# Block attention and a gated MLP on one core: tokens turned by VectorE, row numbers loaded for four query blocks at once, and a new table for the order

## The chip, the cores and the metric

One core of a Trainium2 chip runs the whole program. The metric is the device time of one execution in microseconds (us); less is better. Times of the kernel before are a median of three runs. The profile is one execution, and its trace gives every instruction's engine, source line, start and length.

## What is computed

The reference, cut to what matters (4 batches, 8 heads, 768 tokens, 64 per head; blocks of 32 tokens; 512 model columns, 2048 hidden):

```python
mask = np.abs(blk_i - blk_j) <= 1
mask = mask | (blk_i == 0) | (blk_j == 0) | (blk_i == n_blocks - 1) | (blk_j == n_blocks - 1)
for qb in range(n_blocks):
    for kb in sampled_blocks[qb]:          # three drawn blocks of keys for each block of queries
        mask[qb*32:(qb+1)*32, kb*32:(kb+1)*32] = True
attn = softmax(where(mask, q @ k.T / 8, -1e9)) @ v
x = attn, heads side by side                # 3072 x 512
h = x @ w_in
g = h * np.tanh(np.where(h > 20.0, h, np.log1p(np.exp(np.minimum(h, 20.0)))))
out = g @ w_out
```

The weights arrive as 64-bit floats and are read as pairs of 32-bit words.

## The kernel before, in words

**The work.** Attention goes in 52 jobs, 13 for each batch: one job for query block 0, one for block 23 (these two are dense, they see all keys) and eleven of two neighbouring query blocks each. A job of two blocks runs like this, by the functions in `attend` and around it. `gather_k` copies the keys of the three drawn blocks, whose numbers are only known when the program runs, into the tile `kg` (POOL or ACT, line 588 or 590). `gather_v` fetches the rows of v from the DRAM tensor `vd` into the tile `vg` by DMAs that SyncE (SP) issues (lines 607 to 613). PE multiplies the scores `s` (line 650 in batch 0, which is computed in 32-bit floats; line 660 in the others, where each number is two 16-bit halves). DVE takes their maxima `mx` (line 703), ACT the exponentials `pt` (line 729). The probabilities are turned, by PE in batch 0 (`t`, line 749) and by a transposing DMA in the others (line 784), after a split into halves `p` (lines 773, 775, 780). PE multiplies with v into `o` (lines 814, 830) and DVE divides by the sums into `xs` (lines 851 to 866).

**The turn of the tokens.** `xs` holds 32 queries of four pairs of heads in its 128 partitions. For the MLP the 512 columns have to lie in partitions. Before, `tx_fn` (line 884) does this with one PE product by the identity for each query block, into a PSUM tile `tx`; ACT copies it to 16 bits (`xh`, line 902) and DVE writes what is left (`xl`, line 905).

**The MLP.** Twelve tiles of 256 tokens. PE multiplies `h` from `xh`, `xl` and the split weights `wi` (line 1083; 12 instructions make one unit, 192 units in all) and `y` from `g` and `wo` (line 1143; 6 instructions make one unit, 192 in all). Between them stand, on `[128, 1024]` tiles, the copy `hs` (ACT, line 1092), exponential, square and logarithm `us` (lines 1106 to 1115; the square on POOL, line 1112, or ACT, line 1113), the product `hs` (DVE, line 1116), its 16-bit half `g` (line 1124 or 1122) and the rest of it (POOL, line 1127, or DVE, line 1129). A tile of `h` needs `xh` and `xl` of eight query blocks: job 4 of a batch completes its first tile, job 8 the second, job 12 the third.

**The row numbers.** `blocks_at` (line 562) loads numbers of drawn blocks from an SBUF table into registers of the engine that needs them, by a TENSOR_LOAD (line 567), and keeps them while the next call asks for the same group. A group is one job: two query blocks, six numbers. Each of POOL, ACT and SP has registers of its own.

**What sets the order.** `Plan` (line 41) lists all tasks with their engines, assumed durations, the tiles they read and write and a number `key`. `emit` goes through them as a list scheduler: it takes the task that can start first and, among those that start within 0.02 us, the one with the least ready time plus key. Some tasks have several engines and go to the one that would be done first by the plan. MLP products go in a fixed order of their own. `START` gives the first 18 jobs a time before which their scores count as late, and `RES` an amount of MLP work to be kept for the end. In idle time that the plan foresees on PE in the first 150 us it puts products of zeros (line 918). What each engine executes is then this order, in sequence: an instruction that waits holds up all behind it on its engine. Tiles are taken from rings of fixed size (`RINGS`); PSUM ring `t` has two places, shared by `t`, `tx` and small sums.

## Time and profile before

| | us |
|---|---|
| median of 3 runs | 736.8 |
| lowest and highest of them | 735.41, 741.06 |
| the profiled execution | 739.81 |
| its span in the trace | 737.8 |
| PE, DVE, ACT, POOL busy in the span | 695.8, 577.3, 517.1, 269.9 |

The span runs from the first to the last instruction that the profiler recorded. Busy time counts an engine's instructions without gaps and without waits; register loads, branches and the issuing of DMAs are not in it. "Idle before, releaser" names what ended the wait ahead of an instruction. SPq, ACTq and POOLq are the engines' instruction queues. PEclk is the granted clock of TensorE as a share of 2.4 GHz.

### The profile page before, as it was taken

The page shows a single profiled execution, that of the slowest core. Times are in us where ns is not written, and L with a number is a line of the kernel's source. Part 1 is how long each engine was busy: PE and PEld are TensorE (multiplying, and loading weights), DVE is VectorE, ACT ScalarE, POOL GpSimd, SP SyncE. Part 2 cuts the span into 40 slices and gives each one's busy share as a digit, 9 for nine tenths or more (in the row PEclk, how much of TensorE's full clock was granted, in tenths as well). Part 3 has the DMA queues.
Part 4 walks back from the last instruction along what each step waited for, and adds up shares of the span by engine and source line. Part 5 has one row for each costly group of instructions (what it writes and reads, how often), then busy time and mean ns, then how long its engine had stood idle before and what let it go on. Part 6 is the DMA issues. An engine that isn't in the chain of part 4 may idle for free.

```text
span 737.8 us, 25470 instructions
## 1 busy us (share of the span) xinstructions
PE 695.8 (94%) x10462; PEld 462.3 (63%) x10462; DVE 577.3 (78%) x1064; ACT 517.1 (70%) x841; POOL 269.9 (37%) x330
## 2 busy tenths in 40 slices
PE   9988898999999799998999999998999999999997
PEld 3645776775565376765567666665666666676653
DVE  3788899789988567896969999999899887354350
ACT  3466697998888658877558888877677876464550
POOL 2264453554436232462427554355433511000000
...
GB/s 273 365 207 246 263 208 245 139 132 30 204 145 146 185 154 168 126 238 167 123 135 158 135 215 208 141 187 203 130 175 139 116 137 137 167 65 15 15 15 28
DMA packets 144599, 115.94 MB, mean 157 GB/s; under 512 B 96739, under 2 KB 107492, under 8 KB 144484
## 3 DMA queue, kind: packets, MB, share of 16 engines
q1 hardware_dynamic: 144288, 114.06, 61.5%
...
q14 instruction: 33, 0.27, 0.1%
q10 hardware_dynamic: 196, 0.27, 0.1%
...
## 4 chain that ended last, share of the span: by engine, by line
PE 53%; DVE 17%; DMA 14%; SPq 6%; ACT 5%; issue 4%; POOL 0%; ACTq 0%; DVEq 0%
PE y L1143 22%; PE h L1083 20%; DMA vg<-vd 8%; DMA wr<-in_moe_w_in_dram 3%; PE s L660 3%; PE o L830 3%; SPq L613 3%; DVE p L780 2%; DVE p L775 2%; DVE hs L1116 2%; DMA raw_q<-in_q_dram 2%; DVE mx L703 2%; PE o L814 1%; SPq L567 1%; PE tx L884 1%
## 5 line engine op out<-in xcount | busy, mean ns | idle before, releaser
L1083 PE MATMUL h<-xh,wi 128*128 128x256 f16 x1536 | 284.0, 274 | 0.0
L1143 PE MATMUL y<-wo,g 128*128 128x512 f16 x1152 | 277.4, 382 | 3.6 <-DVE ys L1156 3.6
L1083 PEld LDWEIGHTS <-wi 128*128 128x128 f16 x2304 | 222.5, 98 | 52.8 <-issue 3.4
L1083 PE MATMUL h<-xl,wi 128*128 128x256 f16 x768 | 210.0, 273 | 0.0
L1143 PEld LDWEIGHTS <-g 128*128 128x128 f16 x1152 | 111.0, 99 | 111.0 <-issue 9.8
L588 POOL COPY kg<-kt 128x256 f16 (+1 forms) x213 | 106.6, 542 | 112.7 <-PE s L660 82.3
L729 ACT ACTIVATE pt<-s,nb,ns 128x256 f32<-128x256 f32 (+1 forms) x208 | 105.4, 577 | 4.1 <-DVE nb L718 1.9
L1127 POOL TENSOR_TENSOR g<-hs,g 128x1024 f16<-128x1024 f32 x30 | 67.5, 2250 | 110.6 <-DVE g L1124 39.1
L1092 ACT ACTIVATE hs<-h,gsc 128x512 f32<-128x512 f32 x96 | 65.5, 684 | 59.3 <-PE h L1083 58.8
L1116 DVE SCALAR_TENSOR_TENSOR hs<-us,hs 128x1024 f32<-128x1024 f32 x48 | 61.6, 1284 | 22.5 <-ACT us L1115 22.1
L1112 POOL TENSOR_TENSOR us<-us 128x1024 f32<-128x1024 f32 x27 | 53.5, 1980 | 67.5 <-DVE us L1110 62.2
L780 DVE SCALAR_TENSOR_TENSOR p<-pt,p 128x512 f16<-128x512 f32 (+1 forms) x102 | 73.5, 749 | 1.4 <-ACT p L773 0.6
L775 DVE TENSOR_SCALAR p<-pt 128x512 f16<-128x512 f32 (+1 forms) x68 | 49.0, 740 | 11.5 <-ACT pt L729 8.2
L703 DVE TENSOR_REDUCE mx<-s 128x4 f32<-128x1024 f32 x44 | 53.3, 1212 | 4.8 <-PE s L650 3.0
L1106 ACT ACTIVATE us<-hs,hsc 128x1024 f32<-128x1024 f32 x48 | 55.2, 1151 | 1.3
L1114 ACT ACTIVATE us<-us 128x1024 f32<-128x1024 f32 x48 | 50.7, 1057 | 4.7 <-POOL us L1112 4.0
L1110 DVE TENSOR_SCALAR us<-us 128x1024 f32<-128x1024 f32 x48 | 34.1, 710 | 23.0 <-ACT us L1106 23.0
L1115 ACT ACTIVATE us<-us 128x1024 f32<-128x1024 f32 x48 | 50.7, 1056 | 0.9
L830 PEld LDWEIGHTS <-pp 128*32 128x32 f16 x2952 | 33.6, 97 | 24.4 <-issue 14.0
L830 PE MATMUL o<-vg,pp 128*32 128x65 f16 (+2 forms) x2568 | 36.0, 205 | 9.0 <-DMA vg<-vd 8.7
L590 ACT ACTIVATE kg<-kt 128x256 f16 (+1 forms) x51 | 15.6, 368 | 33.3 <-POOL kg L588 9.8
L918 PE MATMUL zeros<-z 128*128 128x512 f16 x136 | 35.0, 405 | 4.0 <-issue 2.3
...
## 6 DMA issues: line engine op xcount, KB each, us to landing
...
```

The source lines that it names most:

```text
L588: nc.gpsimd.tensor_copy(out=dst, in_=src)
L703: nc.vector.tensor_reduce(out=mx.rearrange("p g w -> p (g w)"), in_=tl[ks].rearrange("p g (w k) -> p (g w) k", k=KT), axis=AX.X, op=ALU.max)
L729: ex = lambda o, x, g, w: nc.scalar.activation(out=o, in_=x, func=AF.Exp, bias=nb[:, g, w:w + 1], scale=ns(w)[:, 0:1])
L775: nc.vector.tensor_scalar(out=h16[:, cs], in0=src, scalar1=PSC, scalar2=None, op0=ALU.mult)
L780: nc.vector.scalar_tensor_tensor(out=x[:, 1, cs], in0=src, scalar=PSC, in1=x[:, 0, cs], op0=ALU.mult, op1=ALU.subtract)
L830: nc.tensor.matmul(o[cs, at] if v1 == VW else o[cs, at, 0:v1 - v0], p[:, k, g, cs], x, start=j == 0 and g == 0 and k == 0 and n == 0, stop ...
L1083: nc.tensor.matmul(h[:, f2].rearrange("p (s q) -> p s q", q=BS), wi[:, fp, w, cc, fs], x[:, :, cc], start=f2 == 0 and k == 0, stop=f2 == 1 ...
L1092: nc.scalar.activation(out=tl[kq][:, 2 * (fp % 2):2 * (fp % 2) + 2], in_=tl[kh], func=AF.Copy, scale=gsc[:, fp:fp + 1])
L1106: nc.scalar.activation(out=new(sb, "us", ku, [P, 4, TT]), in_=hs(), func=AF.Exp, scale=hsc[:, b:b + 1])
L1116: add("DVE", 1.32, lambda: nc.vector.scalar_tensor_tensor(out=hs(), in0=us(), scalar=-0.5, in1=hs(), op0=ALU.add, op1=ALU.mult), r=[ku], w ...
L1127: add("POOL", 2.3, lambda: nc.gpsimd.tensor_tensor(out=g()[:, 1], in0=hs(), in1=g()[:, 0], op=ALU.subtract), r=[kq, ("gh", b, t, k)], w=[k ...
L1143: nc.tensor.matmul(tl[ky], tl["g", b, t, k][:, g, f, q], wo[:, fc, w], start=fc == 0 and n == 0, stop=fc == NFC - 1 and n == 2)
```

## The change

Five things change.

- `tx_fn` is now one DVE instruction for a job (STREAM_TRANSPOSE, turning each block of 32x32), from `xs` into an SBUF tile `tx` with a ring of one place. A column of the 512 ends in another partition than before, and `load_i` takes the rows of w_in in the matching order. The ring of `xs` has one place instead of two.
- `xh` may be made by ACT, POOL or DVE, `xl` by POOL or DVE, as the plan finds it.
- `blocks_at` loads the numbers of four query blocks (12 registers) at once, the last group of a batch two; a group now serves two jobs.
- Every key is looked up in a table `PRIO` by task and batch; `START` and `RES` have other numbers.
- The plan's assumed durations are others, and compute tasks get a small latency by engine (`LAT`).

```diff
-             xs=2, hs=3, us=3, g=4, ys=1, kt=1, q=2, ssk=2, ssv=2, ssq=2, sck=2, scv=2, scq=2, iv=2, ns=3, ws=2,
-             wq=2, am=2, p16=3)
+             xs=1, hs=3, us=3, g=4, ys=1, kt=1, q=2, ssk=2, ssv=2, ssq=2, sck=2, scv=2, scq=2, iv=2, ns=3, ws=2,
+             wq=2, am=2, p16=3, tx=1)
+PRIO = {
+    "zeros": (-1475,),
...
+    "tx": (-80.3, 357.3, -117, -301.3),
...
+}
+def K(name, n):
+    row = PRIO[name]
+    return row[min(n, len(row) - 1)]
+LAT = {"ACT": 0.11, "DVE": 0.08, "POOL": 0.06}
...
+        lat = lat or LAT.get(eng, 0.0)
...
-            n = 2 * NR
+            n = min(4, NB - 1 - qb) * NR
...
         def tx_fn():
-            tx = new(ps["t"], "t", ("tx", i), [P, nsu, P])
-            for w in range(nsu):
-                nc.tensor.transpose(tx[:, w], tl["xs", i][:, w].rearrange("p g d -> p (g d)"), ident)
-        add("PE", 0.25, tx_fn, r=[("xs", i)], w=[("tx", i)], new=[("t", ("tx", i))], key=-3 + (-63 if b == 0 else -7), lat=0.25, kind=("X", i))
+            tx = new(sb, "tx", ("tx", i), [P, nsu, NCC, BS])
+            xs = tl["xs", i].rearrange("p w g d -> p w (g d)").rearrange("p w (d c) -> p w c d", c=NCC)
+            nc.vector.transpose(tx if nsu > 1 else tx[:, 0], xs if nsu > 1 else xs[:, 0])
+        add("DVE", 0.45 if nsu > 1 else 0.3, tx_fn, r=[("xs", i)], w=[("tx", i)], new=[("tx", ("tx", i))], key=K("tx", b))
...
-            run(lambda x, hi, lo: nc.scalar.activation(out=hi, in_=x, func=AF.Copy))
-
-        def xl_fn():
-            run(lambda x, hi, lo: nc.vector.tensor_tensor(out=lo, in0=x, in1=hi, op=ALU.subtract))
+            if eng == "ACT":
+                run(lambda x, hi, lo: nc.scalar.activation(out=hi, in_=x, func=AF.Copy))
+            else:
+                run(lambda x, hi, lo: (nc.vector if eng == "DVE" else nc.gpsimd).tensor_copy(out=hi, in_=x))
+
+        def xl_fn(eng):
+            run(lambda x, hi, lo: (nc.vector if eng == "DVE" else nc.gpsimd).tensor_tensor(out=lo, in0=x, in1=hi, op=ALU.subtract))
...
-        src = w_in.rearrange("(c p) f -> p c f", p=P)[:, :, k * 2 * P * W:(k + 1) * 2 * P * W]
+        src = w_in.rearrange("(p c) f -> p c f", p=P)[:, :, k * 2 * P * W:(k + 1) * 2 * P * W]
...
-            su["first"] = job["sus"][0]["qb"]
+            su["first"] = su["qb"] - (su["qb"] - 1) % 4
...
-    RES, START = 152, [75, 143, 351, 1, 289, 59, 444, 40, 4, 303, 106, 133, 87, 206, 53, 166, 65, 18]
+    RES, START = 142.9, [0, 2.2, 0.9, 28.4, 939.4, 56.8, 14.9, 34.5, 18.6, 102, 75.8, 71.8, 144.1, 1792, 50.5, 27.1, 193.2, 56.8]
```

Where instructions stand, at three places. In a name, `s_17` is the score tile of job 17, `tx_14` the turned tokens of job 14, `h_0_2_3` piece 3 of tile 2 of batch 0; a number at the end counts buffers.

PE in batch 1, behind the scores of job 17, before:

```order
L660 LDWEIGHTS q_1_1_3804
L660 MATMUL s_17_4148<-kg1_110,q_1_1_3804 32x256
L884 MATMUL tx_14_4202<-ident_64,xs_14_4123 128x128 x2
L1143 LDWEIGHTS g_0_1_0_3305
L1143 MATMUL y_0_1_1_4096<-wo_72,g_0_1_0_3305 128x512
```

and now:

```order
L756 LDWEIGHTS q_1_1_3624
L756 MATMUL s_17_4126<-kg1_110,q_1_1_3624 32x256
L1244 LDWEIGHTS g_0_1_2_3534
L1244 MATMUL y_0_1_0_3839<-wo_72,g_0_1_2_3534 128x512
...
L1184 LDWEIGHTS wi_71
L1184 MATMUL h_0_2_3_4008<-xh_0_2_2307,wi_71 128x256
```

The 96 products `tx` are gone from PE's sequence, 9 of which stood ahead of the first MLP product. Job 17's scores now stand at MLP unit 60 of 384, before at unit 68.

SP, from the gather of v for job 4 (its first block goes to `vg0`, its second to `vg1`), before:

```order
L607 DMA vg0_111<-vd0_60 96x520
L567 TENSOR_LOAD offv_87
...
L607 DMA vg1_112<-vd0_60 96x520
...
L931 DMA wor_0_1196<-in_moe_w_out_dram 128x1024
L931 DMA wor_1_1203<-in_moe_w_out_dram 128x1024
L931 DMA wor_2_1255<-in_moe_w_out_dram 128x1024
L931 DMA wor_3_1259<-in_moe_w_out_dram 128x1024
```

and now:

```order
L703 DMA vg0_111<-vd0_60 96x520
...
L1032 DMA wor_0_1189<-in_moe_w_out_dram 128x1024
L1032 DMA wor_1_1197<-in_moe_w_out_dram 128x1024
L1032 DMA wor_2_1234<-in_moe_w_out_dram 128x1024
L1032 DMA wor_3_1238<-in_moe_w_out_dram 128x1024
L1032 DMA wor_4_1250<-in_moe_w_out_dram 128x1024
L1032 DMA wor_5_1279<-in_moe_w_out_dram 128x1024
L703 DMA vg1_112<-vd0_60 96x520
```

Job 4 needs no load of its own any more (job 3's serves it), and six pieces of w_out of 512 KB each are issued between the fetches for its two blocks.

DVE, around the division and the turn of job 4, which completes the first tile of x, before:

```order
L945 SCALAR_TENSOR_TENSOR wi_71<-wr_7_895,wi_71 128x1024
L851 TENSOR_SCALAR r_4_1308<-o_4_1205,iv_r_114 128x4
L855 RECIPROCAL r_4_1308<-r_4_1308 128x4
L866 TENSOR_TENSOR xs_4_1311<-o_4_1205,r_4_1308 128x256
L939 TENSOR_SCALAR wo_72<-wor_0_1196 128x512
```

and now:

```order
L1159 TENSOR_SCALAR hsc_81<-gmx_77,iv_x_78 128x1
L1043 SCALAR_TENSOR_TENSOR wo_72<-wor_4_1250,wo_72 128x512
L1046 SCALAR_TENSOR_TENSOR wo_72<-wor_1_1197,wo_72 128x512
L1040 TENSOR_SCALAR wo_72<-wor_5_1279 128x512
L947 TENSOR_SCALAR r_4_1527<-o_4_1256,iv_r_114 128x4
L951 RECIPROCAL r_4_1527<-r_4_1527 128x4
L962 TENSOR_TENSOR xs_4_1530<-o_4_1256,r_4_1527 128x256
L980 STREAM_TRANSPOSE tx_4_1572<-xs_4_1530 128x256
```

Before, job 4's division followed the last decode of w_in at once; now it stands behind the scales of the MLP (`hsc` is the last of them) and three more instructions that decode w_out.

## Rows read from the trace of the kernel before

**Rows 1.** The chain of work that ended last, its shares by line.
```profile
PE y L1143 22%; PE h L1083 20%; DMA vg<-vd 8%; DMA wr<-in_moe_w_in_dram 3%; PE s L660 3%; PE o L830 3%; SPq L613 3%; DVE p L780 2%; DVE p L775 2%; DVE hs L1116 2%; DMA raw_q<-in_q_dram 2%; DVE mx L703 2%; PE o L814 1%; SPq L567 1%; PE tx L884 1%
```

**Rows 2.** Stretches: length, then busy us of each engine, PEclk, DMA share, GB/s.
```profile
0.00:79.70 79.70, 67.23 (x1092) 39.77 (x1093) 57.83 (x124) 43.59 (x87) 31.88 (x52) 0.97 0.85 271
79.70:140.00 60.30, 55.83 (x1045) 44.48 (x1046) 53.53 (x99) 48.45 (x80) 24.68 (x25) 0.98 0.74 228
140.00:640.00 500.00, 478.95 (x7596) 319.22 (x7595) 430.44 (x795) 382.42 (x628) 213.35 (x255) 0.99 0.68 155
sum 738.00, PE 695.84 PEld 462.25 DVE 577.33 ACT 517.06 POOL 269.92; mean PE 173.96 PEld 115.56 DVE 144.33 ACT 129.27 POOL 67.48
...
400.00:480.00 80.00, 77.90 (x1229) 52.91 (x1228) 77.89 (x140) 66.84 (x112) 39.48 (x37) 1.00 0.77 172
```

**Rows 3.** The same stretches, PE line 884 alone: the sum.
```profile
sum 738.00, PE 20.63 PEld 11.70; mean PE 5.16 PEld 2.92
```

**Rows 4.** PE in order of time, 236 to 262 us: start, length, instructions.
```profile
240.17 4.05 PE L1143 MATMUL y<-wo,g 128*128 128x512 f16 x18
...
250.63 0.69 PE L884 MATMUL tx<-ident,xs 128*128 128x128 f32 x2 [1.49 <-DVE xs L861]
251.11 5.33 PE L1143 MATMUL y<-wo,g 128*128 128x512 f16 x12
```

**Rows 5.** Instructions on the tile tx: ns min/median/max.
```profile
L902 ACT ACTIVATE xh<-tx x60: 255/363/412, 36.4 to 661.2; 128x256 f16<-128x256 f32 x36, 128x128 f16<-128x128 f32 x24
L905 DVE TENSOR_TENSOR xl<-tx,xh x60: 269/410/426, 37.1 to 661.6; 128x256 f16<-128x256 f32 x36, 128x128 f16<-128x128 f32 x24
```

**Rows 6.** Groups by line and shape: busy us, mean ns | idle before.
```profile
L1129 DVE TENSOR_TENSOR g<-hs,g 128x1024 f16<-128x1024 f32 x18 | 22.0, 1224 | 0.5
L775 DVE TENSOR_SCALAR p<-pt 128x512 f16<-128x512 f32 x46 | 37.2, 818 | 11.1 <-ACT pt L729 7.9 <-DMA pp<-p 3.1
L590 ACT ACTIVATE kg<-kt 128x256 f16 x33 | 11.3, 405 | 17.9 <-PE s L660 8.2 <-issue 3.2 <-PE o L830 2.2
L1113 ACT ACTIVATE us<-us 128x1024 f32<-128x1024 f32 x21 | 22.2, 1056 | 8.6 <-DVE us L1110 8.3
L1112 POOL TENSOR_TENSOR us<-us 128x1024 f32<-128x1024 f32 x27 | 53.5, 1980 | 67.5 <-DVE us L1110 62.2 <-DVE iv_x L396 3.8 <-DVE iv_k L396 1.6
L1127 POOL TENSOR_TENSOR g<-hs,g 128x1024 f16<-128x1024 f32 x30 | 67.5, 2250 | 110.6 <-DVE g L1124 39.1 <-ACT g L1122 31.8 <-PE o L830 11.3
```

**Rows 7.** DVE line 775 and ACT line 773: ns min/median/max.
```profile
L775 DVE TENSOR_SCALAR p<-pt x68: 278/424/2256, 176.6 to 624.2; 128x512 f16<-128x512 f32 x46, 128x256 f16<-128x256 f32 x22
...
L773 ACT ACTIVATE p<-pt x34: 399/621/647, 178.3 to 625.3; 128x512 f16<-128x512 f32 x20, 128x256 f16<-128x256 f32 x14
```

**Rows 8.** The register loads of line 567: ns min/median/max.
```profile
L567 POOLq TENSOR_LOAD <-offk x44: 1384/1388/2469, 7.9 to 584.4; - x44
L567 SPq TENSOR_LOAD <-offv x44: 1264/1286/2340, 35.3 to 647.8; - x44
L567 ACTq TENSOR_LOAD <-offk x17: 1324/1337/2686, 8.7 to 598.2; - x17
```

**Rows 9.** DVE in order of time, 58 to 84 us.
```profile
71.07 0.42 DVE L866 TENSOR_TENSOR xs<-o,r 128x256 f32<-128x256 f32 x1
...
77.86 0.20 DVE L1058 TENSOR_SCALAR hsc<-gmx,iv_x 128x1 f32<-128x1 f32 x1
```

**Rows 10.** PE in order of time, 58 to 84 us.
```profile
75.09 0.27 PE L1083 MATMUL h<-xh,wi 128*128 128x256 f16 x1
...
78.35 0.32 PE L814 MATMUL o<-vg,pp 128*32 128x65 f32 x8 [1.79 <-DMA vg<-vd]
...
79.61 0.39 PE L1083 MATMUL h<-xh,wi 128*128 128x256 f16 x1
```

**Rows 11.** The chain between 40 and 84 us, in order of time.
```profile
66.01 1.14 PE s L650 x62
67.15 0.59 PE t L749 x4
...
73.28 5.51 DMA vg<-vd
```

More of the change, by code (lines that the diff above doesn't have):

```diff
@@ L381, in diag @@
                                            accum_out=out())
-        add("DVE", 0.4, diag, r=[kg], w=w, new=new_, key=cls + 12)
+        add("DVE", 0.4, diag, r=[kg], w=w, new=new_, key=K("diag " + ring, 0))
     def root_pe(key, ss, apart):
@@ L437, in load @@
         add("SP", 0.5 * n, fn, r=after, w=keys,
-            new=[(ring, key) for key in keys], key=(-5 if b == 0 else 0) + (0 if b == 0 else 59), lat=1.8,
+            new=[(ring, key) for key in keys], key=K("load " + what, j if b == 0 else len(T3)), lat=1.8,
             kind=("dma", 1.5 * n, n))
@@ L448, in fn @@
             squares(tl["raw", what, b, j], tl[key][:, k:k + 1])
-        add("ACT", 1.28, fn, r=[("raw", what, b, j)], w=[key], new=[(f"ss{what}", key)] if first else (), key=cls + 47 + (19 if b == 0 else 19))
+        add("ACT", 1.05, fn, r=[("raw", what, b, j)], w=[key], new=[(f"ss{what}", key)] if first else (), key=K("ss " + what, j if b == 0 else len(T3)))
     def scales(b, what, j, cls):
@@ L532, in fn @@
                 (nc.vector if eng == "DVE" else nc.gpsimd).tensor_copy(out=dst, in_=src)
-        add("POOL", 0.3, ends, w=[("ends",) + key], new=[("raw", key)], use=[key], key=-2)
-        add("DVE", 0.8, lambda: fn("DVE"), r=[kr, ("ends",) + key], w=[key], use=[key], key=ATV + 94, port=True,
-            also=[("ACT", 1.16, lambda: fn("ACT")), ("POOL", 2.0, lambda: fn("POOL"))])
+        add("POOL", 0.3, ends, w=[("ends",) + key], new=[("raw", key)], use=[key], key=K("ends0", 0))
+        add("DVE", 0.67, lambda: fn("DVE"), r=[kr, ("ends",) + key], w=[key], use=[key], key=K("copy v", j), port=True,
+            also=[("ACT", 1.05, lambda: fn("ACT")), ("POOL", 1.05, lambda: fn("POOL"))])
     def store_v(b, j):
@@ L719, in nb_fn @@
                                             op0=ALU.mult)
-        add("ACT", 0.25 * len(wq), lambda: nb_fn("ACT"), r=[kmx] + NS, w=[("nb", i)],
-            new=[("nb", ("nb", i))], key=45.5 + (21 if b == 0 else -20), also=[("DVE", 0.35 * len(wq), lambda: nb_fn("DVE"))])
+        add("ACT", 0.19 * len(wq), lambda: nb_fn("ACT"), r=[kmx] + NS, w=[("nb", i)],
+            new=[("nb", ("nb", i))], key=K("nb", b), also=[("DVE", 0.15 * len(wq), lambda: nb_fn("DVE"))])
         def ex_fn(n):
@@ L738, in attend @@
         for n in range(2):
-            add("ACT", 1.7 if dense and n == 0 else 1.15, lambda n=n: ex_fn(n),
+            add("ACT", 1.33 if dense and n == 0 else 0.91, lambda n=n: ex_fn(n),
                 r=[kmx, ("nb", i), ks] + (k2 if dense else []) + NS,
-                w=[("p", i, n)], new=[("pt", k) for k in kps] if n == 0 else (), use=kps, key=-1.5 + (-3 if b == 0 else 54))
+                w=[("p", i, n)], new=[("pt", k) for k in kps] if n == 0 else (), use=kps, key=K("ex", b))
         def t_fn(j):
@@ L1053, in fn @@
             nc.vector.tensor_scalar(out=gsc, in0=iv_i, scalar1=rg, scalar2=-2.0 * GSC, op0=ALU.mult, op1=ALU.mult)
-        add("DVE", 0.7, fn, r=[("iv", k) for k in range(0, NFP, 2)], w=["gsc"], key=27)
+        add("DVE", 0.7, fn, r=[("iv", k) for k in range(0, NFP, 2)], w=["gsc"], key=K("gsc", 0))
     def scales_b(b):
@@ L1093, in hs_fn @@
                                  scale=gsc[:, fp:fp + 1])
[L1094 to L1095 removed]
+        add("ACT", 0.58, hs_fn, r=[kh, "gsc"], w=[("hsw", b, t, fp)],
+            new=[("hs", kq)] if fp % 2 == 0 else (), use=[kq], key=K("hs", b))
         if fp % 2 == 1:
@@ L1201, in attn_mish_kernel @@
     add("ACT", 1.0, lambda: which(new), w=["off", "z"],
-        new=[("raw", ("z",))], key=-6, lat=6.0)
+        new=[("raw", ("z",))], key=K("which", 0), lat=6.0)
     globals_(0)
@@ L1259, in attn_mish_kernel @@
         if i == LAST:
-            add("PE", 0.0, spare.clear, r=["zeros", ("begun", i)], use=[("zeros",)], key=-982)
+            add("PE", 0.0, spare.clear, r=["zeros", ("begun", i)], use=[("zeros",)], key=K("clear", 0))
         if b + 1 < B:
```

217 lines of the change are left out of this document (141 added, 76 removed), and 16 rows, old and new, of the table PRIO.

## The prediction

> **What bounds the kernel now.** I read the chain of work that ended last first, then the busy time of each engine by stretches, then single places in order of time, then groups of instructions and register loads. In the chain the reader is to see that the two MLP products of PE hold 42% of the span and that no line of DVE or ACT holds over 2% [rows 1]. The stretches say the same [rows 2]: from 140 to 640 us PE is busy 478.95 of 500, so it idles 21.0; from 79.7 to 140 it idles 4.5; in the first 79.7 us it works on little but prepared weights, the first jobs and zeros while DMA moves 271 GB/s. PE is the bound from its first MLP product on. DVE is the next: 57.8 + 53.5 + 430.4 = 541.8 us busy up to 640, and 77.89 of 80 between 400 and 480, where PE nevertheless has 77.90 of 80 [rows 2]. ACT has 474.5 of 640. So a microsecond taken from PE is worth nearly a microsecond as long as DVE and ACT can deliver the same work in a shorter time.
>
> **The change part by part.** The sum is made against the profiled execution: 739.8 us, that is the span of 737.8 and 2.0 around it. The median of the runs is 736.8, 3.0 lower; I move every result by that.
>
> *The turn leaves PE.* Line 884 takes 20.63 us of PE [rows 3] in 96 products, 0.215 each. Nine stand ahead of the first MLP product, where PE has time to spare; the other 87 stand where PE is the bound: 87 x 0.215 = 18.7 us less. Nothing on PE takes their place, all its other products keep their number except 17 more zeros ahead of the MLP. I take the whole 18.7.
>
> *Waits ahead of the turn leave PE too.* PE executes in order, so a turn that waits for DVE's division holds up the MLP products behind it. At 250.63 it waited 1.49 us, and the 12 `y` products behind it took 5.33 us, where 18 took 4.05 just before, which is 2.70 for 12: 2.63 more [rows 4]. This place alone costs 4.1 us. The others are short, and the wait may come back at a product `h` that needs the last `xl`; but the places of job 17's scores show that jobs now run some 8 MLP units ahead of where they ran. I take 4 us less; the ends are 0 and 8, twice this place.
>
> *What DVE gets.* 44 turns of 256 columns and 8 of 128. No row shows this operation. The nearest rows are `xl` on the same elements, 0.410 and 0.269 at the median and the least [rows 5]: 44 x 0.410 + 8 x 0.269 = 20.2 us. From below I bound it by 52 x 0.278, the least of line 775 [rows 7], 14.5; from above by 52 x 0.818, the mean of its wide form [rows 6], 42.5. I take 20.2, the row with the same shape. A turn can't cost less than nothing on an engine that didn't have it. Against it, `xl` goes to POOL in 53 of 60 cases: 31 x 0.410 + 22 x 0.269 = 18.6 less. The new order also gives DVE 14 more of line 1129 (32 for 18), 14 x 1.224 = 17.1 more [rows 6], takes 11 wide and 8 narrow of line 775 away, 11 x 0.818 + 8 x 0.278 = 11.2 less [rows 6, 7], and adds 8 `xh`, 8 x 0.41 = 3.3 more. The other differences go both ways, none over 5 us; I count them nothing. DVE: 20.2 - 18.6 + 17.1 - 11.2 + 3.3 = 10.8 more, 552.6 of about 620 us, 89%. This lies beside PE's work and costs nothing while that cover holds.
>
> On VectorE's turn the Trainium skill (VectorE: DVE Perf Modes, section on the three transpose paths) has 311 ns for 128x128 in 16 bits, and blocks of 32x32 only. By that, as an estimate, the 96 blocks would be 29.9 us, and DVE would be 20.5 us up instead of 10.8; no run here shows its price, and the forecast stays the same by either.
>
> What DVE may get back: the wide form of line 775 takes 0.818 on average, while the median of both forms is 0.424 and the longest 2.256 [rows 6, 7]; POOL's long operations take 1.98 and 2.25 [rows 6]. An operation of 0.4 that takes the time of POOL's looks like one that had to wait for it: 46 x 0.394 = 18.1 us in this group. Of those POOL operations 27 are left of 57 (lines 1112 and 1127: 11 and 16, before 27 and 30). I count no gain, but this is a reason why DVE should not become the bound.
>
> *What POOL and ACT get.* POOL loses 16 x 1.98 + 14 x 2.25 = 63 us and 75 copies of keys and gains 88 short operations on 256 columns at most; at even 0.8 each they are 70. It has 270 of 738 and isn't near the end of any wait that PE sees. ACT gets the 75 copies, 75 x 0.405 = 30.4 more, 16 squares, 16 x 1.056 = 16.9 more [rows 6], 19 scalings that DVE gave up, 19 x 0.621 = 11.8 more [rows 7], and 43 fewer `xh`, 26 x 0.363 + 17 x 0.255 = 13.8 less [rows 5]. That is 45.3 more: 519.8 before the last job ends. Hidden at 84% of 620 us, with what follows.
>
> *Register loads.* POOL and ACT now have 23 each, SP 24; before 44, 17 and 44. A load of six numbers takes 1.388, 1.337 and 1.286 us [rows 8] and the engine issues nothing in that time. A load of twelve isn't in the trace: between the same time (the cost is that of one access) and twice that (it is by the number). At the same time SP saves 20 x 1.286 = 25.7 us and ACT loses 6 x 1.337 = 8.0. At twice, SP has 24 x 2.57 = 61.7 for 56.6 and ACT 23 x 2.67 = 61.5 for 22.7. Behind a load on SP stand fetches of v that PE waits for: 8% of the chain is that DMA and 1% the load itself [rows 1]. I take the middle, nothing gained or lost: half of the jobs are free of the load and the other half pay more. The ends: 5 us less (the load's share in the chain, 1% of 738, of which half goes) to the rival below.
>
> *The start.* The first MLP product now needs more. Job 4's division stood at 71.07 [rows 9] and the first product came 4.0 us later, at 75.09; after one unit PE waited for job 5's v and went on with `h` at 79.61 [rows 10], so the MLP began, in effect, at 79.6 - 1.3 = 78.3. Now the division stands behind `hsc`, which ended at 78.06 [rows 9], and three decodes of some 0.4 to 0.8 us. That makes xs about 80.1 and the first product 84.1, 5.8 later. Ahead of it PE has then done more: job 7's scores, 1.14, both turns of job 6, 2 x 0.59 [rows 11], and half a product of job 5, 0.3: 2.6 us. 5.8 - 2.6 = 3.2; I take 3 us more. The ends: 2 less, if the two loads saved ahead of job 4's fetch on SP (2 x 1.286) pull the whole start; 6 more, if its second fetch waits behind six pieces of w_out, 6 x 0.524 MB at 271 GB/s = 11.6 us (a fetch behind four took 5.51 [rows 11]): 71.07 + 11.6 + 4.0 - 78.3 - 2.6 = 5.8.
>
> *The rest of the order* (keys, START, RES, places in the rings `xs` and `tx`) I can't price line by line. A single `tx` and a single `xs` bind a job's division to the `xl` of the job before, some 10 us earlier in the MLP stages; I count nothing.
>
> The sum: -18.7 - 4 + 3 = -19.7. 739.8 - 19.7 = 720.1 for an execution like the profiled one, 717 beside the median of 736.8.
>
> **The rivals.**
>
> *A: the order fills PE's gaps as well.* For it: jobs come earlier by some 8 units, so a late fetch of v finds PE with work. Against it: fetches are bound by the release of `vg`, which the change leaves as it was. If half of the 21.0 us of idle time goes, 717 - 10.5 = 706.5.
>
> *B: DVE becomes the bound between 400 and 560.* For it: 97% in rows 2. Against it: PE is at 97% there too, and POOL's long operations get rarer. The stretch is 160 of 560 us of MLP, 0.29. If DVE sets it, PE's gain there is lost, 0.29 x 18.7 = 5.4, and DVE's additions come on top, 0.29 x (10.8 + 22.3, the dearest turn) = 9.6: 717 + 15 = 732.
>
> *C: the loads of twelve cost twice, and ACT stands in the way.* This ends slower. ACT's queue then has 45.3 + 38.8 = 84 us more before the last job ends: 519.8 + 61.5 = 581 of 620, 94%, with loads of 2.67 us in front of exponentials and of the copies `hs` that free PE's tile of `h`. If 0.4 of the 84 shows up as waits of PE, 717 + 34 = 751; it decides from 0.23 on, where the gain of 19.7 is used up. For it: 1.29 to 1.39 us for six numbers is 0.21 to 0.23 for each. Against it: no line of ACT stands in the chain among those that hold 1% or more, and 142 us of ACT's time up to 640 were free. The Trainium skill (Runtime: NRT & Kernel Launch, section on instruction fetch mechanics) says about 200 ns a register even in bulk. By that rule the loads alone would be as in this rival; the trace agrees as far as six registers go and has no other size.
>
> **How the numbers follow.** My forecast, 717, has 0.65, A 0.15, B 0.12, C 0.08. A measurement of this kernel tells about 1%, 7.4 us, from no change, so faster means under 729.4. The forecast's own range comes from its ends: 717 - (2 + 3 + 4 + 1) = 707 with start and waits at their good ends and a little of the loads, 717 + 3 + 4 + 3 = 727 with start and waits at their bad ends and three for DVE. For 8 in 10 I go down to 703, into A, and up to 733, past B; outside are C and the rims, some 0.18. Faster: 0.65 + 0.15 less 0.02 for the forecast's upper rim, 0.78; same: 0.12 + 0.02 = 0.14; slower: 0.08.
>
> **What would show it.** Right, if PE's busy time falls by about 20 us less what 17 zeros add, PE's idle time from its first MLP product to the last stays within some 5 us of 25.5, the first product stands near 84 and the rest of the span is shorter by about 23. The turn's mean on DVE should be near 0.4, and the mean of line 775's successor well under 0.8. Wrong, if PE's idle time grows by as much as its busy time shrinks: with DVE over 95% from 400 to 560 it is B, with loads near 2.7 us and PE waiting for ACT it is C. If idle time in the middle falls by ten it is A.

## The result and the profile after

The change made the kernel slower: 746.3 us, median of four runs (743.91 to 748.38), against 738.5, median of four runs of the kernel before. The ratio is 1.0102 (95% interval 1.0062 to 1.0142). A second comparison, with 12 runs, gave 743.4 us and 1.0073 (1.0040 to 1.0106). The forecast was 717 us.

Stretches of the changed kernel, in the columns of [rows 2], cut at its first MLP product:

```profile
0.00:84.60 84.60, 71.90 (x1163) 41.35 (x1164) 61.90 (x125) 44.67 (x101) 35.73 (x49) 0.96 0.86 270
84.60:140.00 55.40, 47.42 (x835) 37.07 (x831) 47.67 (x88) 41.39 (x71) 18.05 (x26) 0.97 0.71 216
140.00:640.00 500.00, 472.49 (x7638) 314.52 (x7639) 415.54 (x804) 413.70 (x690) 181.30 (x237) 0.99 0.68 157
400.00:480.00 80.00, 77.10 (x1220) 51.05 (x1222) 67.60 (x129) 69.49 (x120) 27.13 (x34) 1.00 0.76 177
```

PE idles 8.0 us between its first MLP product and 140 (4.5 in [rows 2]) and 27.5 from 140 to 640 (21.0). VectorE isn't full: 67.60 of 80 between 400 and 480, where it had 77.89. The chain of work that ended last, by engine (before, then after) and by line after [rows 1]:

```profile
PE 53%; DVE 17%; DMA 14%; SPq 6%; ACT 5%; issue 4%; POOL 0%; ACTq 0%; DVEq 0%
```

```profile
PE 40%; ACT 22%; DVE 14%; DMA 10%; issue 8%; POOL 3%; ACTq 3%; SPq 0%; POOLq 0%; DVEq 0%
PE y L1244 18%; PE h L1184 16%; ACT pt L825 4%; DMA vg<-vd 3%; ACTq L663 2%; PE s L756 2%; ACT us L1215 2%; PE o L926 2%; DMA pp<-p 2%; ACT hs L1193 2%; ACT us L1216 2%; ACT kg L686 2%; DMA raw_q<-in_q_dram 2%; ACT us L1207 2%; ACT us L1214 2%
```

The two MLP products had 42% of the chain and have 34% now. ACT's lines stand in it, and with them ACTq L663: the register load on ACT. The loads of all three engines (ns min/median/max), which answer to [rows 8]:

```profile
L663 SPq TENSOR_LOAD <-offv x24: 1279/2482/3337, 38.4 to 643.3; - x24
L663 POOLq TENSOR_LOAD <-offk x23: 1387/2806/5472, 7.5 to 600.3; - x23
L663 ACTq TENSOR_LOAD <-offk x23: 1329/2619/4135, 9.6 to 601.3; - x23
```

Twelve registers take twice what six took. How such a load can reach PE is to be seen at the place where an MLP product waits longest. First the chain between 225 and 262 us (start, length, what):

```profile
242.90 1.06 ACT us L1216
243.96 3.08 ACTq L663
...
247.51 0.70 ACT kg L686 x2
248.21 0.57 ACT hs L1193
...
249.47 0.57 ACT pt L825
...
250.06 0.64 ACT p L869
...
250.72 0.69 DVE p L876
...
252.84 0.64 DVE tx L980
...
253.53 1.02 POOL xh L1000 x2
254.56 0.83 POOL xl L1003
...
255.43 2.50 PE h L1184 x11
```

ACT stands still for 3.08 us. Behind the load come copies of keys, a copy `hs`, exponentials and a half `p`; DVE waits for that `p` with a finished job's division and turn behind it; POOL then makes `xh` and `xl` in 1.02 and 0.83 us; and only then can PE go on with `h`. The same place by stretches of 2 us:

```profile
248.00:250.00 2.00, 1.34 (x7) 0.49 (x5) 0.00 (x0) 1.97 (x5) 1.06 (x1) 1.00 0.22 61
250.00:252.00 2.00, 0.00 (x0) 0.00 (x0) 1.24 (x5) 1.94 (x5) 0.00 (x0) 0.86 0.67 179
252.00:254.00 2.00, 0.00 (x0) 0.00 (x0) 1.86 (x6) 1.97 (x3) 0.47 (x1) 0.50 0.78 171
254.00:256.00 2.00, 0.94 (x4) 0.50 (x4) 1.75 (x4) 0.88 (x2) 1.77 (x4) 0.50 0.51 100
256.00:258.00 2.00, 2.00 (x18) 1.17 (x23) 0.00 (x0) 1.94 (x3) 0.00 (x0) 0.50 0.98 216
```

PE idles 0.66 + 2 + 2 + 1.06 = 5.7 us, and the wait costs more than itself: while PE stands still the granted clock falls from 1.00 to 0.50 (1.2 GHz), and the 18 products from 256 to 258 still run at that. Over the whole run the mean clock is 0.984, before 0.991. This place is one example; the runs below show that the loss doesn't stand here alone.

The turn and what follows it, on the tile `tx` (ns min/median/max), beside [rows 5]:

```profile
L1003 POOL TENSOR_TENSOR xl<-tx,xh x53: 425/676/1649, 36.6 to 658.0; 128x256 f16<-128x256 f32 x31, 128x128 f16<-128x128 f32 x22
L980 DVE STREAM_TRANSPOSE tx<-xs x52: 401/642/695, 34.9 to 656.8; 128x256 f32<-128x256 f32 x44, 128x128 f32<-128x128 f32 x8
L1000 POOL CAST xh<-tx x35: 291/437/1639, 35.3 to 645.6; 128x256 f16<-128x256 f32 x19, 128x128 f16<-128x128 f32 x16
```

By shape, the turn, DVE's rest of `g` and the successor of line 775 [rows 6] (busy us, mean ns):

```profile
L1230 DVE TENSOR_TENSOR g<-hs,g 128x1024 f16<-128x1024 f32 x32 | 39.2, 1224 | 0.5
...
L980 DVE STREAM_TRANSPOSE tx<-xs 128x256 f32<-128x256 f32 x44 | 28.5, 648 | 1.9 <-DVE xs L959 0.5
...
L871 DVE TENSOR_SCALAR p<-pt 128x512 f16<-128x512 f32 x35 | 19.5, 560 | 16.7 <-ACT pt L825 13.5 <-DMA pp<-p 3.2
...
L980 DVE STREAM_TRANSPOSE tx<-xs 128x128 f32<-128x128 f32 x8 | 3.3, 408 | 0.5
```

The theories, as the runs were set up. 1: long register loads give the gain back. 2: the new order and its sharing of work lose it. 3: the turn on VectorE, with single places for `xs` and `tx`, delays x. Later: 4, order and start; 5, VectorE has no room for the turn; 6, the turn on PE was worth less than 18.7 us; 7, VectorE sets the time as much as PE. The unchanged kernel ran beside every experiment; ratios are to it, and 0.1% is 0.74 us. All experiments on the loads, and those on one row's price, keep every other row of every engine in its place, because the plan doesn't see what was edited.

### The profile page after: what moved, and what is told of

Same layout as the page of the kernel before. It is cut to its first block, busy times and chain, and to the rows that moved or that the text cites. A ratio compares the mean times of both kernels' runs of the same rounds, so it can differ in the third digit from the quotient of the medians.

```text
span 742.0 us, 25358 instructions
## 1 busy us (share of the span) xinstructions
PE 689.9 (93%) x10383; PEld 454.0 (61%) x10383; DVE 562.5 (76%) x1065; ACT 545.7 (74%) x908; POOL 238.1 (32%) x314
## 4 chain that ended last, share of the span: by engine, by line
PE 40%; ACT 22%; DVE 14%; DMA 10%; issue 8%; POOL 3%; ACTq 3%; SPq 0%; POOLq 0%; DVEq 0%
PE y L1244 18%; PE h L1184 16%; ACT pt L825 4%; DMA vg<-vd 3%; ACTq L663 2%; PE s L756 2%; ACT us L1215 2%; PE o L926 2%; DMA pp<-p 2%; ACT hs L1193 2%; ACT us L1216 2%; ACT kg L686 2%; DMA raw_q<-in_q_dram 2%; ACT us L1207 2%; ACT us L1214 2%
## 5 line engine op out<-in xcount | busy, mean ns | idle before, releaser
L684 POOL COPY kg<-kt 128x256 f16 (+1 forms) x138 | 68.2, 534 | 159.0 <-PE s L756 104.1
L1217 DVE SCALAR_TENSOR_TENSOR hs<-us,hs 128x1024 f32<-128x1024 f32 x48 | 59.3, 1237 | 24.0 <-ACT us L1216 23.8
L686 ACT ACTIVATE kg<-kt 128x256 f16 (+1 forms) x126 | 38.5, 372 | 49.1 <-POOL kg L684 17.0
L876 DVE SCALAR_TENSOR_TENSOR p<-pt,p 128x512 f16<-128x512 f32 (+1 forms) x102 | 63.0, 642 | 13.1 <-ACT p L869 12.5
L1000 POOL CAST xh<-tx 128x256 f16<-128x256 f32 (+1 forms) x35 | 22.4, 648 | 122.8 <-DVE tx L980 110.4
L1003 POOL TENSOR_TENSOR xl<-tx,xh 128x256 f16<-128x256 f32 (+1 forms) x53 | 41.8, 795 | 40.8 <-ACT xh L998 29.7
L1215 ACT ACTIVATE us<-us 128x1024 f32<-128x1024 f32 x48 | 50.5, 1055 | 4.9 <-POOL us L1213 4.1
L1214 ACT ACTIVATE us<-us 128x1024 f32<-128x1024 f32 x37 | 39.1, 1056 | 19.6 <-DVE us L1211 19.5
L1216 ACT ACTIVATE us<-us 128x1024 f32<-128x1024 f32 x48 | 50.5, 1054 | 0.8
L1228 POOL TENSOR_TENSOR g<-hs,g 128x1024 f16<-128x1024 f32 x16 | 37.1, 2316 | 36.1 <-DVE g L1225 21.7
L1019 PE MATMUL zeros<-z 128*128 128x512 f16 x153 | 39.2, 404 | 1.7 <-POOL z L1014 1.7
```

The costliest lines, as they stand in the source:

```text
L684: nc.gpsimd.tensor_copy(out=dst, in_=src)
L876: nc.vector.scalar_tensor_tensor(out=x[:, 1, cs], in0=src, scalar=PSC, in1=x[:, 0, cs], op0=ALU.mult, op1=ALU.subtract)
L1214: also=[("ACT", 0.96, lambda: nc.scalar.activation(out=us(), in_=us(), func=AF.Square))])
L1215: add("ACT", 0.97, lambda: nc.scalar.activation(out=us(), in_=us(), func=AF.Ln, bias=1.0), w=[ku], key=K("ln", b))
L1216: add("ACT", 0.97, lambda: nc.scalar.activation(out=us(), in_=us(), func=AF.Exp, scale=-1.0), w=[ku], key=K("un", b))
L1217: add("DVE", 1.15, lambda: nc.vector.scalar_tensor_tensor(out=hs(), in0=us(), scalar=-0.5, in1=hs(), op0=ALU.add, op1=ALU.mult), r=[ku], w ...
```

## Experiments on the register loads

**Two blocks again (new_two).** From the changed kernel:

```diff
-            n = min(4, NB - 1 - qb) * NR
+            n = 2 * NR
...
-            su["first"] = su["qb"] - (su["qb"] - 1) % 4
+            su["first"] = job["sus"][0]["qb"]
```

> The changed kernel, with row numbers loaded for two query blocks at once again (six registers); the order of everything else is the same row for row. Theory 1 (the loads of twelve, about 2.6 us each on SP, POOL and ACT, give back what the turn wins): 720 to 728 us, PE's idle time from 84 to 640 falls from 35.5 to under 25. Theory 2 (the new order and its sharing of work, which puts short operations of ACT ahead of what PE waits for, is the loss): 742 to 748. Theory 3 (VectorE's turn with one place each for xs and tx delays x): as theory 2 here.

Measured: 734.8 us, ratio 0.9940 (0.9903 to 0.9977). PE's idle time from 140 to 640 falls from 27.5 to 19.6:

```profile
140.00:640.00 500.00, 480.43 (x7750) 319.59 (x7751) 423.62 (x816) 420.32 (x695) 184.26 (x239) 0.99 0.67 158
```

Two groups in which PE waited (last column: idle before, releaser), in this kernel:

```profile
L1184 PE MATMUL h<-xh,wi 128*128 128x256 f16 x1536 | 285.8, 275 | 1.3 <-POOL xh L1000 1.2
...
L756 PE MATMUL s<-kg,q 64*32 64x256 f16 x1584 | 29.5, 279 | 3.6 <-ACT pt L825 3.0 <-DVE kg L690 0.6
```

and in the changed kernel:

```profile
L1184 PE MATMUL h<-xh,wi 128*128 128x256 f16 x1536 | 285.8, 275 | 5.0 <-POOL xh L1000 4.9
...
L756 PE MATMUL s<-kg,q 64*32 64x256 f16 x1584 | 29.7, 281 | 6.4 <-ACT pt L825 5.4 <-DVE kg L690 0.9
```

So the long loads cost, but 720 to 728 was not reached: they are a part of the loss, not the whole.

**The same once more (new_two_again).**

> The changed kernel with loads for two blocks everywhere once more, beside the one above and beside the kernel before: 731 to 736 us, 0.3 to 1.0% under the kernel before.

Measured: 737.6 us, 0.9977 (0.9946 to 1.0009), a little over what was expected. Over both comparisons this kernel stands at about 0.996, 3 us under the kernel before; the changed one stands at 1.0088 (mean of 1.0102 and 1.0073). The loads of twelve therefore cost 1.3%, 9.5 us.

**Before with four blocks (old_four).** The edit above the other way round.

> The kernel before, with row numbers loaded for four query blocks at once and nothing else changed, in the order of before row for row. Theory 1: slower, 748 to 760 us. Theories 2 and 3: 735 to 742, since half of the jobs are free of a load and the other half pay twice.

Measured: 742.6 us, 1.0065 (1.0036 to 1.0094). Between the two expectations: 4.8 us. In the old order ACT has 12 long loads, in the new one 23.

**Which engine's loads (new_sp4, new_ap4, after_again).** The changed kernel, with the group's size by engine:

```diff
-        qb = su["first"]
+        four = eng == mybir.EngineType.SP      # new_ap4: !=
+        qb = su["first"] if four else su["qb"] - (su["qb"] - 1) % 2
...
-            n = min(4, NB - 1 - qb) * NR
+            n = min(4 if four else 2, NB - 1 - qb) * NR
```

> The changed kernel with loads for four blocks on SP alone and for two on ACT and POOL; all other rows the same. If the loads on SP, ahead of the fetches of v, are what costs: 742 to 747 us. If it is the loads on ACT and POOL, ahead of exponentials and copies: 733 to 738.

> The changed kernel with loads for four blocks on ACT and POOL and for two on SP. Loads for two everywhere gave 734.8, for four on SP alone 737.8, for four everywhere 746.3. If the rest of the loss stands on ACT and POOL by itself: 741 to 745 us. If it takes the long loads on all three: 735 to 739.

> The changed kernel as it is, beside the three that follow: 740 to 748 us, 0.5 to 1.5% over the kernel before.

Measured: four on SP alone 1.0003 (0.9971 to 1.0035); four on ACT and POOL alone 1.0073 (1.0045 to 1.0102); four everywhere 1.0073 (1.0040 to 1.0106). ACT's and POOL's loads alone carry as much as all three together, about 1.1% over loads for two. SP's fetches of v, which I had looked at most, are not where most of it stands; 1.0003 isn't clear of new_two's 0.996 by the noise, so a small part on SP isn't excluded. PE's idle time from 140 to 640 goes the same way: 18.5 us with four on SP alone, 26.1 with four on ACT and POOL alone:

```profile
140.00:640.00 500.00, 473.90 (x7628) 314.40 (x7627) 414.74 (x808) 416.16 (x693) 178.21 (x240) 0.98 0.67 155
```

At the place shown for the changed kernel, around 254 us, new_ap4 has

```profile
252.92 0.27 PE L1185 MATMUL h<-xh,wi 128*128 128x256 f16 x1 [1.78 <-POOL xh L1001]
254.12 0.27 PE L1185 MATMUL h<-xl,wi 128*128 128x256 f16 x1 [0.92 <-POOL xl L1004]
```

That is 2.7 us of waiting instead of 5.7, at the same ratio of 1.0073; new_sp4 waits 4.1 us there and new_two 2.1. So the loss isn't this one wait. From 140 to 640 PE's scores wait 7.1 us for ACT's exponentials in the changed kernel, 6.1 in after_again and 5.2 in new_ap4, against 3.3 and 2.8 in the two runs with loads for two. Its `y` products wait 4.2 to 4.3 us for ACT's `ys` in those three, against 2.1 and 2.6. The loss is spread over such waits.

**One block (new_one, new_ap1_sp2).** The group is one block everywhere, or one on ACT and POOL and two on SP:

```diff
+        m = 2 if eng == mybir.EngineType.SP else 1     # new_one: 1 for all, written out
+        qb = su["qb"] - (su["qb"] - 1) % m
...
-            n = min(4, NB - 1 - qb) * NR
+            n = m * NR
```

> The changed kernel with row numbers loaded for one query block at a time (three registers; ACT and POOL then load only what they use); all other rows as in the changed kernel. So far: loads for four blocks 746.3, for two 734.8. Theory 1 (an engine that stands still for one long load costs more than for the same registers in short ones): 727 to 732 us. If only the sum of registers or the count of loads mattered, SP with 88 loads: 734 to 742.

> The changed kernel with loads for one block on ACT and POOL (42 and 46 loads of three numbers, 0.71 and 0.73 us each, 21 us less on ACT than with 38 loads of 1.34) and for two on SP. If an engine's loading time counts by its sum on ACT and POOL: 728 to 732 us, under the kernel with loads for two. If it counts only where one load is long: the same as with loads for two, 732 to 736.

Measured: one everywhere 736.9 us, 1.0004 (0.9973 to 1.0036), a miss for theory 1 and inside the other range; one on ACT and POOL only 732.0 us, 0.9902 (0.9868 to 0.9936), beside 0.9977 of new_two_again. That is the fastest version here that leaves nothing out, faster than both kernels; it is clear of new_two_again, but not of new_two's 0.9940. Its loads:

```profile
L664 SPq TENSOR_LOAD <-offv x44: 1264/1287/2857, 38.0 to 632.8; - x44
L664 POOLq TENSOR_LOAD <-offk x46: 723/731/2926, 8.0 to 588.1; - x46
L664 ACTq TENSOR_LOAD <-offk x42: 687/707/2417, 9.8 to 589.1; - x42
```

By the medians, ACT spends 42 x 0.707 = 29.7 us on loads instead of 23 x 2.619 = 60.2 in the changed kernel, because it loads the numbers of the blocks that it serves and no others. Why 88 single loads on SP (0.678 us at the median) take this gain back wasn't found: their sum is 59.7 us against 56.7.

## Experiments on the turn and on PE's price

**The turn alone, planned anew (old_turn).** The kernel before with VectorE's turn, `xs` and `tx` with one place each, `xh` on ACT and `xl` on DVE; the planner places it by the old keys.

```diff
-             xs=2, hs=3, us=3, g=4, ys=1, kt=1, q=2, ssk=2, ssv=2, ssq=2, sck=2, scv=2, scq=2, iv=2, ns=3, ws=2,
-             wq=2, am=2, p16=3)
+             xs=1, hs=3, us=3, g=4, ys=1, kt=1, q=2, ssk=2, ssv=2, ssq=2, sck=2, scv=2, scq=2, iv=2, ns=3, ws=2,
+             wq=2, am=2, p16=3, tx=1)
...
+            nc.vector.transpose(tx if nsu > 1 else tx[:, 0], xs if nsu > 1 else xs[:, 0])
-        add("PE", 0.25, tx_fn, r=[("xs", i)], w=[("tx", i)], new=[("t", ("tx", i))], key=-3 + (-63 if b == 0 else -7), lat=0.25, kind=("X", i))
+        add("DVE", 0.45 if nsu > 1 else 0.3, tx_fn, r=[("xs", i)], w=[("tx", i)], new=[("tx", ("tx", i))], key=-3 + (-63 if b == 0 else -7))
...
```

> The kernel before, with VectorE turning tokens, one place each for xs and tx as in the changed kernel (w_in's rows in the order that this needs), xh on ACT and xl on DVE as before, loads for two blocks; the planner with its old keys sets the order. Theory 1 and theory 2: 718 to 728 us, the 18.7 us that the turn takes from PE. Theory 3: 738 or more, with PE waiting ahead of h for xl.

Measured: 751.7 us, 1.0183 (1.0144 to 1.0222). Slower, but the plan moved other rows too: it has 189 products of zeros instead of 136, and the first MLP product came at 87.7 instead of 75.1. It doesn't tell the turn from its order.

**The new table alone (new_pe_two).** The changed kernel with PE's turn, `xh` on ACT, `xl` on DVE, `xs` with two places, loads for two.

```diff
...
-            nc.vector.transpose(tx if nsu > 1 else tx[:, 0], xs if nsu > 1 else xs[:, 0])
+            for w in range(nsu):
+                nc.tensor.transpose(tx[:, w], tl["xs", i][:, w].rearrange("p g d -> p (g d)"), ident)
-        add("DVE", 0.45 if nsu > 1 else 0.3, tx_fn, r=[("xs", i)], w=[("tx", i)], new=[("tx", ("tx", i))], key=K("tx", b))
+        add("PE", 0.25, tx_fn, r=[("xs", i)], w=[("tx", i)], new=[("t", ("tx", i))], key=K("tx", b), lat=0.25, kind=("X", i))
...
```

> The changed kernel's keys, durations, START and RES alone: the turn is PE's again, through PSUM, xh on ACT, xl on DVE, xs with two places, loads for two blocks. Theory 2: 750 us or more (746 and some of the turn's 18.7 us on PE). Theory 1: 735 or less. Theory 3: 738 or less.

Measured: 794.7 us, 1.0751 (1.0705 to 1.0797). A table of keys made for one set of tasks sets a poor order for another, so this says nothing on the order of the changed kernel; inconclusive. From here on everything else was kept row for row.

**The turn alone, row for row (old_turn_row).** The plan still counts the turn as PE's; what is issued at its place is VectorE's instruction, into the same PSUM ring:

```diff
-            tx = new(ps["t"], "t", ("tx", i), [P, nsu, P])
-            for w in range(nsu):
-                nc.tensor.transpose(tx[:, w], tl["xs", i][:, w].rearrange("p g d -> p (g d)"), ident)
+            tx = new(ps["t"], "t", ("tx", i), [P, nsu, NCC, BS])
+            xs = tl["xs", i].rearrange("p w g d -> p w (g d)").rearrange("p w (d c) -> p w c d", c=NCC)
+            nc.vector.transpose(tx if nsu > 1 else tx[:, 0], xs if nsu > 1 else xs[:, 0])
...
```

> The kernel before, with the turn done by VectorE at the very place where PE's turn stood in the program, from the same xs into the same PSUM ring t; w_in's rows in the order that this needs; every other row of every engine as before. Theory 4 (the new order and its later start cost what the turn wins): 716 to 724 us, since PE loses 87 x 0.215 and a few waits and VectorE's 32 us find room. Theory 5 (the turn's room on VectorE isn't free: with it VectorE, 97% busy from 400 to 480, holds PE): 732 or more, and PE's idle time from 140 to 640 rises from 21 to 35 or more.

Measured: 749.9 us, 1.0192 (1.0149 to 1.0235), 14.2 us over the kernel before. Its stretches, its chain by engine, and a piece of that chain between 440 and 470 us:

```profile
140.00:640.00 500.00, 467.89 (x7443) 307.95 (x7444) 449.29 (x832) 379.53 (x625) 216.43 (x257) 0.98 0.67 153
400.00:480.00 80.00, 73.72 (x1260) 50.27 (x1249) 78.00 (x146) 63.12 (x109) 39.44 (x39) 1.00 0.75 174
```

```profile
PE 37%; DVE 36%; DMA 8%; ACT 7%; issue 6%; SPq 4%; ACTq 0%; POOL 0%; POOLq 0%; DVEq 0%
```

```profile
440.36 0.43 DVE p L780
440.79 0.18 issue
440.96 0.64 DVE tx L884
441.60 0.58 DVE us L1110
442.19 0.65 DVE ys L1156
442.83 0.33 DVE xl L905
443.16 1.28 DVE p L775
444.44 1.13 DVE mx L703
```

PE idles 32.1 us from 140 to 640, 11.1 more than before and a little short of theory 5's 35; the time is in its range. VectorE holds 36% of the chain, before 17%. Between 400 and 480 VectorE was full already (77.89 of 80) and stays full (78.00), and now PE follows it: 73.72 instead of 77.90. The chain there runs from one DVE instruction to the next, and the turn is one of them. Single rings aren't to blame here: `xs` has its two places.

**Relief for VectorE (old_less, old_turn_row_less).** The product that ends `hs` works on half of its columns:

```diff
-            out=hs(), in0=us(), scalar=-0.5, in1=hs(), op0=ALU.add, op1=ALU.mult)
+            out=hs()[:, 0:2], in0=us()[:, 0:2], scalar=-0.5, in1=hs()[:, 0:2], op0=ALU.add, op1=ALU.mult)
```

> The kernel before, the product that ends hs computed on half of its columns (48 of them on VectorE, some 29 us less there, nothing less on PE); all other rows the same. Theory 7 (in the kernel before VectorE sets the time as much as PE does): 724 to 731 us. If PE alone sets it: 734 to 739.

> The kernel before with the turn on VectorE at the place of PE's, and the product that ends hs on half of its columns, so that VectorE has about as much to do as before and PE 96 products less. Theory 7: 722 to 730 us, against 749.9 without the relief. If the turn costs by its place in VectorE's queue (what waits for it or stands behind it) and not by its length: 740 or more.

Measured: old_less 734.2 us, 0.9949 (0.9920 to 0.9978), clear of the kernel before, but just inside the range for PE alone and short of theory 7's; old_turn_row_less 743.1 us, 1.0078 (1.0044 to 1.0112), in the range for the place. The group of `hs` on VectorE goes from 61.6 us to 36.5 and 38.1, some 24 us less, not the 29 expected. That gives 3.8 us to the kernel before and 8.4 to the one with the turn, so VectorE's length counts. But old_turn_row_less has 573.1 us of VectorE in its span, the kernel before 577.3; with that and 96 products less on PE it is still 0.78% slower, 5.8 us (against old_less 0.78 + 0.51 = 1.3%, 9.5 us). So 6 to 9.5 of the 14 us aren't VectorE's length. The likely reason is the turn's place, in the queue of an engine whose next instruction others wait for; no run moved the place alone.

**What a turn on PE is worth (old_twice, old_half).** Each turn done twice, or of a job's two the second left out:

```diff
-            for w in range(nsu):
+            for w in [w for w in range(nsu) for _ in range(2)]:      # old_half: for w in range(1)
...
```

> The kernel before, each turn done twice on PE (96 products more), every other row as before. If PE's time at its full price decides (0.215 each, nine hidden by the start): 754 to 757 us. Theory 6 (the turns fill time in which PE would wait anyway, so the term of 18.7 was too large): 738 to 748.

> The kernel before without 44 of the 96 turns on PE: of a job's two columns of tx the second is left out, and xh and xl read the first one twice; every other row as before. At the full price 40 x 0.215 = 8.6 us less, 727 to 730. Theory 6: 733 to 738.

Measured: old_twice 747.8 us, 1.0136 (1.0092 to 1.0181), 11.0 us more; old_half 737.1 us, 1.0007 (0.9976 to 1.0038), nothing less that can be told from noise (-1.8 to +2.8 us). PE's group of line 884, of which the kernel before has 96 in 20.6 us, in old_twice:

```profile
L884 PE MATMUL tx<-ident,xs 128*128 128x128 f32 x192 | 32.1, 288 | 6.4 <-DVE xs L863 2.9 <-DVE xs L861 1.9 <-DVE xs L866 1.3
```

and in old_half:

```profile
L884 PE MATMUL tx<-ident,xs 128*128 128x128 f32 x52 | 15.4, 297 | 7.0 <-DVE xs L861 3.5 <-issue 1.7 <-DVE xs L863 1.0
```

96 more turns add 32.1 - 20.6 = 11.5 us to the group and 11.0 to the run: 0.115 for each, not 0.215. A lone product shows 0.29, and the 44 second ones add 20.6 - 15.4 = 5.2 us to the group, 0.12 each: the 96 lengths of 0.290 add up to 27.8 us and cover 20.6, so neighbours overlap. The group's busy time isn't what leaves the run when products leave: without those 5.2 us it was no shorter. Both runs change only products that stand behind another. What the 52 first ones give back, 15.4 us of the group and the waits ahead of them, was not tried by itself.

**The same question in the new order (new_two_h96, new_two_half).** new_two with 96 turns of the identity added, one ahead of each tile of `h` (first two lines); and new_two with VectorE turning one of a job's two columns.

```diff
+            if f2 == 0:
+                nc.tensor.transpose(h[:, 0, 0:P], ident, ident)
...
-            nc.vector.transpose(tx if nsu > 1 else tx[:, 0], xs if nsu > 1 else xs[:, 0])
+            nc.vector.transpose(tx[:, 0], xs[:, 0])
...
```

> The changed kernel with loads for two blocks and 96 more products on PE, each a turn of the identity (128x128, float32) into h's tile ahead of a unit of the MLP; the result is not touched. Before, 96 more turns cost 11.0 us. If PE sets the time in the new order: 745 to 748 us. If VectorE and ACT set it: 735 to 740.

> The changed kernel with loads for two blocks, VectorE turning one of a job's two columns of xs (44 turns of 128 columns for 256, 10.6 us less on VectorE), xh and xl reading it twice; all other rows the same. If the turn on VectorE, or the way from xs to xl, holds PE: 724 to 730 us. If not: 732 to 737, as with the whole turn.

Measured: with 96 more, 737.5 us, 1.0010 (0.9972 to 1.0048), which is some 4 us over new_two's 0.996, hardly clear of noise, and inside the range for VectorE and ACT. The added group:

```profile
L1183 PE MATMUL h<-ident 128*128 128x128 f32 x96 | 27.4, 286 | 0.1
```

It shows 27.4 us of busy time and costs about a seventh of that. With half of the turn on VectorE 731.0 us, 0.9906 (0.9868 to 0.9944), 2.5 to 4 us under new_two's two comparisons for 10.6 us of VectorE, between the two ranges; the intervals overlap.

**The start (new_two_vfirst7).** In new_two, the six fetches of w_out ahead of job 4's second fetch of v are issued behind it.

```diff
-            fn()
+            if t in self.hold:            # the fetches of w_out
+                self.held.append(fn)
+            else:
+                fn()
+            if t in self.release:         # job 4's second fetch of v
+                for f in self.held:
+                    f()
+                self.held, self.hold = [], ()
...
```

> The changed kernel with loads for two blocks, and on SP the six fetches of w_out that stand ahead of job 4's second fetch of v moved behind it; all other rows the same. If the later start (first MLP product at 85 instead of 75) costs: 728 to 731 us with the first product at 81 or before. If the start is hidden later: 733 to 737.

Measured: 737.6 us, 0.9991 (0.9951 to 1.0030). No gain, but the edit moved the start the wrong way: in the profiled execution the first MLP product came at 92.4, in new_two at 85.0. From its chain and from PE in order of time:

```profile
76.77 9.12 DMA wor<-in_moe_w_out_dram
...
92.41 0.38 PE L1195 MATMUL h<-xh,wi 128*128 128x256 f16 x1
```

Decodes of w_out stand ahead of job 4's division on VectorE, and now VectorE waits for their fetches. So this run doesn't show what the six fetches, or the later start, cost in the changed kernel; both stay open.

## Why the prediction was wrong, step by step

Its premise, a microsecond taken from PE is worth nearly a microsecond as long as VectorE and ACT can deliver, failed. Leaving 44 products out gave nothing that can be told from noise; adding 96 cost 11.0 us in the old order and some 4 in the new. With all 96 moved to VectorE and every other row in place, the kernel was 14.2 us slower, where the sum has 22.7 less for the turn and the waits ahead of it. PE at 96% was not alone in setting the time; VectorE, full for part of the span, and the queues between them did too.

| term of the sum | forecast | by the runs |
|---|---|---|
| the turn leaves PE, with the waits ahead of it, and costs nothing on VectorE | -22.7 | +14.2 (old_turn_row against before) |
| the rest of the order, with the start | +3 | -17.2 (new_two against old_turn_row) |
| register loads | 0 | +9.5 (changed kernel against new_two) |
| sum | -19.7 | +6.5 |

The measured change is +5.4 to +7.5 us (1.0073 and 1.0102). The right column walks from the kernel before to the changed one over two kernels that were run, so its sum is right by construction; each step is good to some 3 or 4 us, and taken in another sequence the steps could have other prices. The first and the third row are the steps that failed. The second is luck: a gain that the forecast counted at nothing hides more than all of the turn's loss, and no run takes it apart.

- *The turn leaves PE* took 20.63 us of [rows 3] as a price. Doubling gave 0.115 for each, leaving second products out gave nothing, and a job's first product wasn't tried by itself. In the changed kernel PE's whole busy time fell by 5.9 us (695.8 to 689.9), where some 16 were forecast (20.6 less 4.2 for the 17 zeros).
- *Waits ahead of the turn.* They left, and others came: without the long loads PE idles 19.6 us (21.5 in the second run) from 140 to 640, against 21.0.
- *What DVE gets.* The turn was priced at 20.2 us and took 28.5 + 3.3 = 31.8, within its bounds (14.5 to 42.5). That it costs nothing beside PE's work is what failed. The Trainium skill (VectorE: DVE Perf Modes, section on the three transpose paths) led to an estimate of 29.9, which was nearer. Line 775's successor fell from 0.818 to 0.560 on average, as thought. VectorE had 525.1 us up to 640 where 552.6 were forecast, so rival B did not come in this order: 133.8 of 160 us from 400 to 560. It did in the old order (old_turn_row, 154.0 of 160). Against that kernel new_two is 2.3% faster, 17 us: this is what *the rest of the order*, counted at nothing, the new sharing (`xl` on POOL above all) and the turn into SBUF are worth together. They pay for moving the turn and leave 3 us.
- *What POOL and ACT get.* ACT's work was forecast at 519.8 us up to 640 and is 499.8. Hidden at 84% was the wrong test. ACT's share is lower than PE's, but exponentials, copies `hs` and keys go through it in sequence, and its lines now hold 22% of the chain (before 5%, in the line by engine). It is 18% in new_two, so most of this came with the order and not with the long loads. POOL's `xh` and `xl` are short in sum and yet stand right ahead of `h`.
- *Register loads.* "I take the middle, nothing gained or lost" is the other step that failed. Twelve numbers cost twice six, the upper bound; the cost was to be sought on ACT and POOL, not in SP's share of the chain. This was rival C's mechanism, at 9.5 us instead of 34. That C's 751 lies near the measured 746.3 is luck: the loads are a third of the 29 us between the forecast and the result. The small gain named for the loads is half of 1% of 738, which is 3.7 us and not 5; the range took 1 of it. Of register loads the Trainium skill (Runtime: NRT & Kernel Launch, section on instruction fetch mechanics) says about 200 ns a register even in bulk. The traces, with a table in SBUF, agree: 0.71 to 0.73 us for three on ACT and POOL, 1.29 to 1.39 for six, 2.48 to 2.81 for twelve.
- *The start.* The first MLP product was forecast near 84.1 and came at 84.6 (86.7 in after_again). The agreement is luck: job 4's `xs` stood at 82.53 instead of 80.1, because the scales ended 1.6 us later and the division then waited 0.85 for PE's `o`, and from there to the first product it took 2.05 us instead of 4.0. Measured like the forecast, the product is 84.6 - 78.3 - 2.6 = 3.7 us late, and PE idles 8.0 - 4.5 = 3.5 more up to 140; that is 7.2, over the bad end of 6. What of it reaches the end of the run isn't shown. The cause given for the bad end, the six fetches of w_out, stays open, since the run that moved them made the start later.
